# A fused recurrence and mish MLP on one core: 64-column state updates, VectorE low parts for 16 units, and a new planned order

## The chip, the cores and the metric

The kernel runs on one core of a Trainium2 chip. The metric is the device time of one execution in microseconds (us). The kernel before takes 505.66 us, the median of three runs (505.22 to 505.91).

## The reference

The inputs are `q`, `k`, `v` and `f_logit` of shape (batch 4, heads 8, 768 steps, width 48), all float32, and two weight matrices, `w_in` (384 x 2048) and `w_out` (2048 x 384), in float64.

```
f = sigmoid(f_logit)
state = 0                                   # per batch and head, 48 x 48
for t in range(768):
    state = f[t][:, None] * state + outer(k[t], v[t])
    y[t]  = q[t] @ state
x = y as (3072 tokens, 8 * 48 = 384)
h = x @ w_in                                # 3072 x 2048
g = h * tanh(softplus(h))                   # mish
out = g @ w_out                             # 3072 x 384
```

## The kernel before

**The recurrence.** Each sequence is cut into 6 blocks of 128 steps, so with 4 batches there are 24 chunks n = 0 to 23; a chunk holds all 8 heads of one batch. Two heads sit on the 128 partitions, 64 places each: 48 numbers in groups of three, each group followed by an empty place (`places` in the host layout, with zeros for v). A chunk is worked in four steps. `prep`/`attn0` make decays and the masked scores (L449, L455), `attn1` transposes k (by TensorE, or from chunk 8 by VectorE and DMA), `attn2` multiplies transposed k by v to get the chunk's two state updates `u[0]` and `u[1]` (L514) and VectorE adds them to the state (`mid` L534, `tmp` L536), and `attn3` makes the outputs y (L553, L565). `leave` brings y into the token layout `xt` in two parts, a rounded high part and the remainder, and GpSimd decays the state (L588).

**The joined runs.** From chunk 9 (`JOIN`) the scores of a chunk, the outputs of the chunk before it and the state update are one uninterrupted TensorE step of small matmuls, 15 runs in all (n = 9 to 23). There the update uses array tiles of 64 rows x 32 columns, 4 pairs of heads x 4 column groups x 2 halves of the chunk. In the last four (n >= 20) only the first half is needed. Each small float32 matmul shows as two matmul records and two weight loads in the trace. The moving operand of the update is v with the empty places left out, a pattern of 16 groups of 3; the other matmuls of the run (L449, L553, L565) move 64 contiguous columns.

**The MLP.** Tokens are taken in 6 groups of 512, the 2048 hidden features in 16 blocks: 96 units. A unit has 9 matmuls h = xt x w_in (L245; three products of high and low parts for each of three row blocks), an elementwise chain (`mish`), and 9 matmuls o = w_out x g (L271). The chain of a unit: ScalarE L259, VectorE L260, ScalarE L256, L262, L263, VectorE g (L264), ScalarE the high part gh (L265), GpSimd the low part gl = g - gh (L266). Units 0 to 15 are feature blocks 0 to 7 of groups 0 and 1; units 16 to 31 are blocks 8 to 15 of the same groups (`TURNS`). `split_w` turns one block's float64 weights, loaded as pairs of 32-bit words, into high and low parts with ScalarE (L357, L364) and VectorE (L359, L360, L362, L365), one block for each of units 0 to 7 and 16 to 23.

**The order.** Nothing runs at the place where the code names it. Every step is added to `Plan` with its engine, a cost, and what it reads and writes. `order` packs the steps onto five in-order queues by a list schedule, forward and backward in turns (`BASE`: look-ahead, weight of waiting, number of turns), perturbs the ranks with each seed of `SEEDS`, packs once more, and issues all steps in the order of their planned starts. Steps marked `port` (SBUF-only VectorE steps, and all of GpSimd's) are planned so that they do not overlap. `FREE` gives each engine's first free time; the order of its keys decides which engine is taken when two steps could start at the same time. Before the first MLP output, small matmuls on zeros (`idle`, L345) fill planned TensorE gaps.

Of the kernel before, what the change touches and what calls it, by code (L numbers as in the profile page):

```python
# [10 lines left out]
F32 = mybir.dt.float32  # L11
# [3 lines left out]
ALU = mybir.AluOpType  # L15
PSUM = bass.MemoryType.PSUM

B, H, S, D = 4, 8, 768, 48
# [6 lines left out]
NP = H // 2  # L25
NS = 4
GC = B
GT = GC * C
# [11 lines left out]

LEAD = [(-4, 4), (24, 32)]
SEEDS = [
# [4 lines left out]
]  # L47
BASE = (600.0, 20.0, 2)
NR = 3
LAG = 2  # L50
TD = 8
# [1 line left out]
KD_SIZE = 131.0  # L53
RAW = 786
SQ_DVE = ()


class Plan:
# [4 lines left out]

    LATENCY = {"pe": 230.0, "act": 170.0, "dve": 160.0, "pool": 180.0, "sp": 1550.0}
    RATE = 0.385
    FREE = {"pe": 1500.0, "act": 1900.0, "dve": 1200.0, "pool": 2100.0, "sp": 600.0}

    def __init__(self):
        self.steps = []
# [16 lines left out]
    def pack(self, rank, ahead, haste, back=False):  # L86
# [10 lines left out]
        if back:  # L97
            before, after = after, before
        free = dict.fromkeys(self.FREE, 0.0) if back else dict(self.FREE)
        queue = {e: [] for e in free}  # L100
# [54 lines left out]
    def order(self):  # L155
        count = len(self.steps)
        cost = [s[1] for s in self.steps]
        ahead, haste, turns = BASE
        rank = list(range(count))
# [9 lines left out]
    def issue(self):  # L169
        at = self.FREE["pe"]  # L170
        for i in self.order():
            engine, cost, issue = self.steps[i][:3]
            if engine == "pe":

                if self.start[i] <= self.start[self.until]:
                    while at + 527.0 < self.start[i]:
                        self.idle()
                        at += 427.0 if at > 6500.0 else 853.0
                at = self.start[i] + cost
            issue()  # L180
# [8 lines left out]
def T_ACT(n, psum=False, bias=0):  # L189
    return n / 1.2 + (50 if psum else 92) + 93 * bias + 2  # L190


def T_DVE(n):
    return n / 0.96 + 70


def T_POOL(n):
    return n * 2.3 + 60
# [3 lines left out]
def recurrence_moe_kernel(  # L202
# [12 lines left out]
    nc = tc.nc  # L215
# [32 lines left out]
                n += 1  # L248


    def mish(h, n, g, gh, gl, on_dve=False):


        square = (
            ("dve", T_DVE(GT), 1, lambda: nc.vector.tensor_tensor(n, n, n, ALU.mult)) if on_dve else
            ("act", T_ACT(GT), 0, lambda: nc.scalar.activation(n, n, AF.Square))  # L256
        )
        return (
            ("act", T_ACT(GT, True), 0, lambda: nc.scalar.activation(n, h, AF.Exp)),  # L259
            ("dve", 70 + GT / 1.92, 1, lambda: nc.vector.tensor_scalar(n, n, U_CAP, 1.0, ALU.min, ALU.add)),  # L260
            square,
            ("act", T_ACT(GT, False, 1), 0, lambda: nc.scalar.activation(n, n, AF.Ln, bias=ones)),  # L262
            ("act", T_ACT(GT), 0, lambda: nc.scalar.activation(n, n, AF.Exp, scale=-1.0)),  # L263
            ("dve", 662, 0, lambda: nc.vector.scalar_tensor_tensor(g, n, half_, h, ALU.subtract, ALU.mult)),  # L264
            ("act", T_ACT(GT), 0, lambda: nc.scalar.activation(gh, g, AF.Copy)),  # L265
            ("pool", T_POOL(GT), 1, lambda: nc.gpsimd.tensor_tensor(gl, g, gh.bitcast(F32), ALU.subtract)),  # L266
        )

# [7 lines left out]
    with tc.tile_pool(name="work", bufs=1) as pool, tc.tile_pool(  # L276
        name="psum", bufs=1, space=PSUM
    ) as psum:
        def ring(name, n, shape, dtype=F32, space=pool):
            return [space.tile(shape, dtype, tag=f"{name}{i}", name=f"{name}{i}") for i in range(n)]  # L280
# [9 lines left out]
        n_, g_ = (ring(nm, 2, [P, GT]) for nm in "ng")  # L290
        gh_, gl_ = (ring(nm, 3, [P, GT], F32R) for nm in ("gh", "gl"))
# [3 lines left out]
        at_, h_, o_ = (ring(nm, n, [P, GT], F32, psum) for nm, n in (("at", 3), ("h", 2), ("o", NK)))  # L295
# [41 lines left out]
        at1, zeros = at_[2], o_[NK - 1]  # L337
# [87 lines left out]
        def half(e):  # L425
            return slice(64 * e, 64 * e + 64)
# [4 lines left out]
        def real(x):  # L431
            return x.rearrange("x p (r m) -> x (p r) m", m=4)[:, :, 0:3]
# [59 lines left out]
        def attn2(n):  # L492
            last = n >= NCH - B
            st, ks = state[:, n % B], ("st", n % B)
            v = v_[n % NR]
            join = n >= JOIN
            u = [x[:, c : c + NP * D].rearrange("p (a c) -> p a c", a=NP) for x, c in ((at1, 0), (at_[1], NP * 64))]
            keys = [("at", 2), ("at", 1)]
            if join:
                u.reverse()  # L500
                keys.reverse()
            flat = [x.rearrange("x p (r m) -> x (p r) m", m=3) for x in u]
            (mid, mk), (tmp, tk) = ((r[n % 2], (nm, n % 2)) for nm, r in (("mid", mid_), ("tmp", tmp_)))

            kt = kt_[n % 2]

            def update():
                m = 32 if join else 64
                for p in range(NP):
                    for r in range(0, P, m):  # L510
                        for c in range(2 - last):
                            c0 = 2 * p * 64 + r // 64 * 64
                            moving = v[half(c), c0 : c0 + 64].rearrange("x (r m) -> x r m", m=4)[:, :, 0:3]
                            nc.tensor.matmul(u[c][r : r + m, p, :], kt[half(c), p, r : r + m], moving, start=True, stop=True)  # L514

            if join:
                scores, mask, reads, writes = late[n]
                outputs, qreads, after = ahead[n - 1]
                add("pe", 2300, lambda: [scores(), outputs(), update()], [("kt", n % 2), ("v", n % NR)] + reads + qreads,
                    [("at", b) for b in range(3)])  # L520
                after()
                mask()
            elif n >= GC:
                scores, mask, reads, writes = late[n]
                add("pe", 1190, lambda: [update(), scores()], [("kt", n % 2), ("v", n % NR)] + reads,
                    list(dict.fromkeys(keys[: 2 - last] + writes)))
                mask()
            else:
                add("pe", 640, update, [("kt", n % 2), ("v", n % NR)], keys[: 2 - last])
            if n < B:  # L530
                add("act", T_ACT(NP * D, True), lambda: nc.scalar.activation(real(mid), flat[0], AF.Copy),
                    keys[:1], [mk])
            else:
                add("dve", T_DVE(NP * D), lambda: nc.vector.tensor_tensor(real(mid), real(st), flat[0], ALU.add), keys[:1] + [ks], [mk])  # L534
            if not last:
                add("dve", T_DVE(NP * D), lambda: nc.vector.tensor_tensor(real(tmp), flat[1], real(mid), ALU.add), keys[1:] + [mk], [tk])  # L536
# [79 lines left out]


        steps = (attn0, attn1, attn2, attn3)

        def attend():  # L620
# [75 lines left out]
        for u in range(len(units) + LAG):  # L696
            if u < len(units):
                t, g, j = units[u]
                if j == split:
                    split_w(j)  # L700
                    split += 1
                x, hs, us, gs = g % 2, u % 2, u % 2, u % 3
                xk = [(hl, ("xt", x, c), p) for hl in "hl" for c in range(GC) for p in range(NK)]
                h = h_[hs]
                add("pe", 2050, lambda h=h, x=x, j=j: moe_in(h, xt_[x], j), xk + [("w", "h", j), ("w", "l", j)], [("h", hs)])
                kh, kn, kg = ("h", hs), ("n", us), ("g", us)
                ops = mish(h, n_[us], g_[us], gh_[gs], gl_[gs], u in SQ_DVE)
                rw = (
                    ([kh], [kn]), ([], [kn]), ([], [kn]), ([], [kn]), ([], [kn]),
                    ([kh, kn, "half_"], [kg]), ([kg], [("gh", gs)]), ([kg, ("gh", gs)], [("gl", gs)]),  # L710
                )
                for (e, c, shared, fn), (r, w) in zip(ops, rw):
                    add(e, c, fn, r, w, port=shared)
            while done < min(4 * NCH, attend_goal(u) + 3 * (JOIN < NCH)):
                attend()
            if u == len(units):
                check()
            if u >= LAG:
                out_unit(u - LAG)
# [8 lines left out]
    with tc.If(good < total):  # L728
# [3 lines left out]
        with tc.tile_pool(name="slow", bufs=1) as pool, tc.tile_pool(  # L732
            name="slow_psum", bufs=1, space=PSUM
        ) as psum:
            def st(shape, name):
                return pool.tile(shape, F32, tag=name, name=name)
# [5 lines left out]
            with tc.For_i(0, B, 1) as b:  # L742
                with tc.For_i(0, NP, 1) as p:
# [15 lines left out]
                    with tc.For_i(0, D, 1) as e:  # L759
                        v = st([P, S], "sv")  # L760
# [24 lines left out]
            with tc.For_i(0, NG, 1) as g:  # L785
                x = st([P, NK, GT], "sx")
# [10 lines left out]
                n, g_ = (st([P, GT], nm) for nm in ("sn", "sg"))  # L797
                gh, gl = (pool.tile([P, GT], F32R, tag=nm, name=nm) for nm in ("sgh", "sgl"))
# [87 lines left out]
```

## Time and profile before

| What | Value |
|---|---|
| Median of 3 runs | 505.66 us |
| The profiled execution, its own time | 507.56 us |
| Its span, first to last instruction | 505.8 us |
| Mean granted TensorE clock, as a share of full speed | 0.990 |
| TensorE matmul busy | 485.6 us (96%) |
| ScalarE busy | 396.9 us (78%) |
| VectorE busy | 304.1 us (60%) |
| GpSimd busy | 155.2 us (31%) |

In the profile PE is TensorE's matmuls, PEld its weight loads, DVE VectorE, ACT ScalarE, POOL GpSimd and SPq the queue of SyncE that issues the transfers. The profile's times count from the first instruction. Busy shares are averages over stretches with different limits, so the rows further down are taken stretch by stretch.

### The profile page before, as it was taken

To read this page: it belongs to the slowest core of one execution; us is meant where nothing else is said; L and a number is where in the kernel's file an instruction comes from. 1 tells how busy PE (TensorE), PEld (TensorE's weight loads), DVE (VectorE), ACT (ScalarE), POOL (GpSimd) and SP (SyncE) were. 2 spreads that over 40 slices of the span, in tenths; PEclk is the share of its full clock that TensorE was granted. 3 is DMA by queue.
4 is the path that set the end of the run, shared out by engine and by line. 5 is a ranking of instruction groups with operands and counts; after the bars stand their busy time and mean duration, and the time that the engine had idled before them with its cause. 6 is when DMAs were issued, how large, how long until landed. Compare 5 with 4: busy or idle time off the path is not lost.

```text
span 505.8 us, 13416 instructions
## 1 busy us (share of the span) xinstructions
PE 485.6 (96%) x5594; PEld 394.0 (78%) x5594; DVE 304.1 (60%) x512; ACT 396.9 (78%) x714; POOL 155.2 (31%) x138
## 2 busy tenths in 40 slices
PE   7998999998999989999999999999999999999995
PEld 5766777776788877888888888888888888888883
DVE  3997999999846855577466366456365433233221
ACT  6996998888998876498877878877877777777680
POOL 3121354332433313142322332322332333342421
PEclk8998999999999999999999999999999999999998
DMA  8876556453142462643233252233141100100001
GB/s 300 305 259 220 182 183 194 153 172 131 48 145 61 125 182 76 194 110 75 74 86 101 69 153 74 69 75 100 50 134 22 24 32 1 43 21 1 0 1 67
DMA packets 55379, 54.53 MB, mean 108 GB/s; under 512 B 36976, under 2 KB 38128, under 8 KB 55312
## 3 DMA queue, kind: packets, MB, share of 16 engines
q1 hardware_dynamic: 55312, 53.63, 34.8%
q8 instruction: 44, 0.72, 0.6%
q14 instruction: 23, 0.19, 0.1%
HBM read 40.76 MB, written 10.49 MB: 101 GB/s over the span
## 4 chain that ended last, share of the span: by engine, by line
PE 76%; DVE 10%; ACT 7%; issue 3%; DMA 1%; POOL 1%; SPq 1%; DVEq 0%; ACTq 0%; POOLq 0%
PE o L271 34%; PE h L245 33%; PE at L514 2%; PE at L565 2%; PE at L449 2%; DVE wt L362 2%; PE at L553 2%; DVE g L264 1%; DVE wt L360 1%; DVE kq L312 1%; DVE wl L365 1%; DVE n L260 1%; DVE cum L409 1%; ACT wt L357 1%; DVE wt L359 1%
## 5 line engine op out<-in xcount | busy, mean ns | idle before, releaser
L266 POOL TENSOR_TENSOR gl<-g,gh 128x512 fp32r<-128x512 f32 x96 | 131.3, 1369 | 299.0 <-ACT gh L265 268.0
L245 PE MATMUL h<-xt,wh 128*128 128x512 f32 x576 | 181.3, 396 | 7.6 <-DVE g L264 4.8
L245 PEld LDWEIGHTS h<-xt,wh 128*128 128x128 f32 x576 | 107.2, 189 | 34.0 <-DVE g L264 8.8
L264 DVE SCALAR_TENSOR_TENSOR g<-n,half,h 128x512 f32<-128x512 f32 x96 | 71.4, 744 | 74.9 <-ACT n L263 68.5
L271 PE MATMUL o<-gh,wh 128*128 128x512 f32 x288 | 114.0, 396 | 0.0
L245 PE MATMUL h<-xt,wl 128*128 128x512 f32 x288 | 112.7, 391 | 0.0
L271 PE MATMUL o<-gh,wl 128*128 128x512 f32 x288 | 112.2, 390 | 0.0
L271 PE MATMUL o<-gl,wh 128*128 128x512 f32 x288 | 112.2, 390 | 0.0
L259 ACT ACTIVATE n<-h 128x512 f32<-128x512 f32 x96 | 56.9, 592 | 49.6 <-PE h L245 49.3
L260 DVE TENSOR_SCALAR n<-n 128x512 f32<-128x512 f32 x96 | 44.8, 468 | 70.1 <-ACT n L259 69.7
L256 ACT ACTIVATE n<-n 128x512 f32<-128x512 f32 x96 | 60.5, 630 | 16.6 <-DVE n L260 16.4
L262 ACT ACTIVATE n<-n,ones 128x512 f32<-128x512 f32 x96 | 69.4, 723 | 2.7
L265 ACT ACTIVATE gh<-g 128x512 fp32r<-128x512 f32 x96 | 60.0, 625 | 12.7 <-DVE g L264 10.8
L271 PEld LDWEIGHTS o<-gh,wh 128*128 128x128 f32 x288 | 54.0, 188 | 12.4 <-ACT n L256 0.4
L245 PEld LDWEIGHTS h<-xt,wl 128*128 128x128 f32 x288 | 54.5, 189 | 11.7
L271 PEld LDWEIGHTS o<-gl,wh 128*128 128x128 f32 x288 | 54.1, 188 | 11.5
L271 PEld LDWEIGHTS o<-gh,wl 128*128 128x128 f32 x288 | 54.1, 188 | 10.8
L263 ACT ACTIVATE n<-n 128x512 f32<-128x512 f32 x96 | 60.3, 628 | 1.8
L312 DVE TENSOR_TENSOR kq<-kq,at 128x512 f32<-128x512 f32 (+1 forms) x39 | 26.0, 668 | 2.4 <-ACT at L417 1.4
L409 DVE TENSOR_TENSOR_SCAN cum<-go,l 128x512 f32<-128x512 f32 x20 | 26.1, 1304 | 0.0
L455 DVE TENSOR_TENSOR a<-at,causal 128x256 f32<-128x256 f32 x44 | 17.9, 413 | 13.4 <-PE at L514 13.4
L514 PE MATMUL at<-v,kt 64*32 64x48 f32 (+1 forms) x1120 | 19.5, 214 | 2.6 <-issue 2.6
(104 smaller groups left out, 451.7 us busy)
## 6 DMA issues: line engine op xcount, KB each, us to landing
raw<-ww SPq DMA_DIRECT2D x16, 768.0 KB, 4.9
kq<-kq SPq DMA_DIRECT2D x63, 128.0 KB, 3.2
v<-vn SPq DMA_DIRECT2D x24, 256.0 KB, 3.4
l<-fl SPq DMA_DIRECT2D x20, 256.0 KB, 2.8
out<-ob SPq DMA_DIRECT2D x18, 256.0 KB, 2.9
kd<-inv SPq DMA_DIRECT2D x64, 64.0 KB, 2.2
kt<-kd SPq DMA_DIRECT2D x16, 256.0 KB, 2.7
xt<-xt SPq DMA_DIRECT2D x15, 128.0 KB, 2.1
```

The source lines that it names most:

```text
L245: nc.tensor.matmul(h, w[:, j, a * P : (a + 1) * P], xt[:, x, a, :], start=(n == 0), stop=(n == 3 * NK - 1))
L256: ("act", T_ACT(GT), 0, lambda: nc.scalar.activation(n, n, AF.Square))
L259: ("act", T_ACT(GT, True), 0, lambda: nc.scalar.activation(n, h, AF.Exp)),
L260: ("dve", 70 + GT / 1.92, 1, lambda: nc.vector.tensor_scalar(n, n, U_CAP, 1.0, ALU.min, ALU.add)),
L262: ("act", T_ACT(GT, False, 1), 0, lambda: nc.scalar.activation(n, n, AF.Ln, bias=ones)),
L263: ("act", T_ACT(GT), 0, lambda: nc.scalar.activation(n, n, AF.Exp, scale=-1.0)),
L264: ("dve", 662, 0, lambda: nc.vector.scalar_tensor_tensor(g, n, half_, h, ALU.subtract, ALU.mult)),
L265: ("act", T_ACT(GT), 0, lambda: nc.scalar.activation(gh, g, AF.Copy)),
L266: ("pool", T_POOL(GT), 1, lambda: nc.gpsimd.tensor_tensor(gl, g, gh.bitcast(F32), ALU.subtract)),
L271: nc.tensor.matmul(o, w[:, j, m * P : (m + 1) * P], x, start=(first and i == 0), stop=(last and i == 2))
L312: add("pool" if on_pool else "dve", cost, lambda: eng.tensor_tensor(dst, x, y, ALU.mult), reads, writes, port=port)
L409: add("dve", 2 * T_DVE(w) - 70, lambda s=s, cum=cum: nc.vector.tensor_tensor_scan(cum.rearrange("p a c -> p (a c)"), go[:, s].rearrange("p ...
```

## The change

Four things. (1) In joined runs the update's moving operand is all 64 columns of a head's v, empty places included, the PSUM target is 64 columns wide for each pair, and VectorE reads it back without the empty places. (2) For units 0 to 15 VectorE makes gl in place of GpSimd. (3) In `FREE` GpSimd stands ahead of VectorE, and `BASE` has 6 turns in place of 2. (4) `SEEDS` is another list, of 50 in place of 31, so that the order of all engines' instructions is another one. Planned costs of the joined run (2300) stay as they were.

```diff
-    62000004, 62000073, ...            (31 seeds)
+    71000002, 71000010, ...            (50 seeds)
-BASE = (600.0, 20.0, 2)
+BASE = (600.0, 20.0, 6)
+LOW_DVE = range(16)
-    FREE = {"pe": 1500.0, "act": 1900.0, "dve": 1200.0, "pool": 2100.0, "sp": 600.0}
+    FREE = {"pe": 1500.0, "act": 1900.0, "pool": 2100.0, "dve": 1200.0, "sp": 600.0}
-    def mish(h, n, g, gh, gl, on_dve=False):
+    def mish(h, n, g, gh, gl, on_dve=False, low_on_dve=False):
             ("act", T_ACT(GT), 0, lambda: nc.scalar.activation(gh, g, AF.Copy)),
+            ("dve", T_DVE(GT), 1, lambda: nc.vector.tensor_tensor(gl, g, gh.bitcast(F32), ALU.subtract)) if low_on_dve else
             ("pool", T_POOL(GT), 1, lambda: nc.gpsimd.tensor_tensor(gl, g, gh.bitcast(F32), ALU.subtract)),
-            u = [x[:, c : c + NP * D].rearrange("p (a c) -> p a c", a=NP) for x, c in ((at1, 0), (at_[1], NP * 64))]
+            cols = 64 if join else D
+            u = [x[:, c : c + NP * cols].rearrange("p (a c) -> p a c", a=NP) for x, c in ((at1, 0), (at_[1], NP * 64))]
-            flat = [x.rearrange("x p (r m) -> x (p r) m", m=3) for x in u]
+            flat = [real(x) if join else x.rearrange("x p (r m) -> x (p r) m", m=3) for x in u]
-                            moving = v[half(c), c0 : c0 + 64].rearrange("x (r m) -> x r m", m=4)[:, :, 0:3]
+                            moving = v[half(c), c0 : c0 + 64]
+                            if not join:
+                                moving = moving.rearrange("x (r m) -> x r m", m=4)[:, :, 0:3]
-                ops = mish(h, n_[us], g_[us], gh_[gs], gl_[gs], u in SQ_DVE)
+                ops = mish(h, n_[us], g_[us], gh_[gs], gl_[gs], u in SQ_DVE, u in LOW_DVE)
```

## Rows read from the trace of the kernel before

**Rows 1.** Busy time by stretch: PE, PEld, DVE, ACT, POOL, granted clock, DMA share, GB/s.
```profile
40.00:50.00 10.00, 9.85 (x111) 7.67 (x112) 6.44 (x13) 6.37 (x12) 1.76 (x2) 0.83 0.73 251
50.00:75.00 25.00, 24.96 (x510) 19.61 (x508) 23.63 (x44) 23.89 (x47) 11.31 (x9) 1.00 0.57 186
75.00:131.50 56.50, 51.72 (x457) 39.69 (x438) 54.42 (x70) 47.89 (x81) 20.04 (x14) 1.00 0.51 157
131.50:495.40 363.90, 361.31 (x3840) 298.24 (x3840) 187.50 (x333) 284.51 (x501) 110.34 (x91) 1.00 0.26 73
```

**Rows 2.** What TensorE waited for in all: total us, times, longest.
```profile
PE h L245 <- DVE g L264: 4.8, 9, 0.8
PE h L245 <- DMA xt<-xt: 2.8, 1, 2.8
PE at L514 <- issue: 2.6, 2, 1.5
```

**Rows 3.** Timeline of TensorE's matmuls in the joined run of chunk 15.
```profile
248.28 0.69 PE L449 MATMUL at<-kq 64*64 64x64 f32 x32
...
249.87 0.96 PE L514 MATMUL at<-v,kt 64*32 64x48 f32 x64
...
250.77 0.50 PE L271 MATMUL o<-gh,wh 128*128 128x512 f32 x1
```

**Rows 4.** Line L565 by shape in 249.59 to 249.86 us; line L514 of that run.
```profile
L565 PE MATMUL at<-a,v 64*32 64x64 f32 x32 | 0.5, 222 | 0.0
...
L514 PE MATMUL at<-v,kt x64: 199/203/225, 249.9 to 250.6; 64*32 64x48 f32 x64
```

**Rows 5.** Timeline of the joined run of chunk 20, its update and what follows.
```profile
345.09 0.62 PE L514 MATMUL at<-v,kt 64*32 64x48 f32 x32
345.64 0.50 PE L271 MATMUL o<-gh,wh 128*128 128x512 f32 x1
```

**Rows 6.** Timeline of a joined run with a pause inside its update.
```profile
178.70 0.69 PE L449 MATMUL at<-kq 64*64 64x64 f32 x32
...
180.29 0.64 PE L514 MATMUL at<-v,kt 64*32 64x48 f32 x38
182.41 0.38 PE L514 MATMUL at<-v,kt 64*32 64x48 f32 x26 [1.48 <-issue]
```

**Rows 7.** DMA queues of the page: packets, MB, share of 16 engines.
```profile
q8 instruction: 44, 0.72, 0.6%
```

**Rows 8.** VectorE's groups in 75 to 131.5 us: count, busy us, mean ns.
```profile
L365 DVE TENSOR_TENSOR wl<-wt,wh 128x768 fp32r<-128x768 f32 x7 | 9.8, 1405 | 0.0
L360 DVE SCALAR_TENSOR_TENSOR wt<-raw,wt 128x768 int32<-128x768 int32 x8 | 9.8, 1225 | 0.1
L260 DVE TENSOR_SCALAR n<-n 128x512 f32<-128x512 f32 x12 | 8.5, 712 | 0.0
L362 DVE SCALAR_TENSOR_TENSOR wt<-raw,wt 128x768 int32<-128x768 int32 x7 | 7.7, 1104 | 0.0
L359 DVE TENSOR_SCALAR wt<-wt 128x768 int32<-128x768 int32 x7 | 5.0, 707 | 0.1
```

**Rows 9.** The tiles wl and gl in 40 to 140 us: ns min/median/max.
```profile
L365 DVE TENSOR_TENSOR wl<-wt,wh x12: 927/953/2051, 44.6 to 135.5; 128x768 fp32r<-128x768 f32 x12
L266 POOL TENSOR_TENSOR gl<-g,gh x18: 1297/1342/2218, 50.3 to 137.5; 128x512 fp32r<-128x512 f32 x18
```

**Rows 10.** Timelines of POOL, then DVE, at 82 to 86 us.
```profile
82.87 1.75 POOL L266 TENSOR_TENSOR gl<-g,gh 128x512 fp32r<-128x512 f32 x1 [2.63 <-ACT gh L265]
...
82.52 0.95 DVE L362 SCALAR_TENSOR_TENSOR wt<-raw,wt 128x768 int32<-128x768 int32 x1
83.39 2.05 DVE L360 SCALAR_TENSOR_TENSOR wt<-raw,wt 128x768 int32<-128x768 int32 x1
```

**Rows 11.** VectorE's groups by shape: in 10 to 40 us, in 200 to 495, over the span.
```profile
L359 DVE TENSOR_SCALAR wt<-wt 128x768 int32<-128x768 int32 x5 | 2.8, 554 | 0.1
...
L260 DVE TENSOR_SCALAR n<-n 128x512 f32<-128x512 f32 x64 | 27.3, 427 | 59.7 <-ACT n L259 59.3
...
L312 DVE TENSOR_TENSOR kq<-kq,inv 128x256 f32<-128x256 f32 x2 | 0.8, 421 | 2.9 <-ACT inv L416 2.9
L455 DVE TENSOR_TENSOR a<-at,causal 128x256 f32<-128x256 f32 x44 | 17.9, 413 | 13.4 <-PE at L514 13.4
L534 DVE TENSOR_TENSOR mid<-state,at 128x192 f32<-128x192 f32 x20 | 6.9, 344 | 0.0
```

**Rows 12.** Timeline of TensorE at the first MLP unit.
```profile
40.16 0.74 PE L245 MATMUL h<-xt,wh 128*128 128x512 f32 x2 [2.76 <-DMA xt<-xt]
```

9 rows, old and new, of the table SEEDS are left out of this document.

## The prediction

> **What bounds the kernel now.** I read the page's busy shares first, then the table by stretch, then TensorE's waits, then single joined runs, then VectorE's groups in the one stretch where TensorE starves. The reader is to see four stretches. Up to 40 us the first chunks of the recurrence are worked, and the first MLP matmul starts at 40.16 after a wait for the copy inside xt [rows 12]. From 40 to 75 us TensorE is nearly full while VectorE has 10.00 - 6.44 = 3.6 and 25.00 - 23.63 = 1.4 us idle [rows 1]. From 75 to 131.5 us VectorE is busy 54.42 of 56.50 us and TensorE idles 56.50 - 51.72 = 4.8 us; the release named is VectorE's g, which frees the bank of h [rows 1, 2]. From 131.5 to 495.4 us TensorE is full: 361.31 of 363.90 us, and all but half a microsecond of the rest are two pauses inside state updates that no engine explains, 2.6 us together [rows 1, 2]. VectorE has more than 170 us to spare there. So a microsecond of TensorE work taken out after 131.5 us should arrive at the end whole; a microsecond of VectorE work counts only between 75 and 131.5 us; GpSimd, at 110 of 364 us in the long stretch, counts only through what it holds up.
>
> **The update with 64 columns.** Before, a run's update is 64 matmul records, from 249.87 to the next matmul at 250.77: 0.90 us [rows 3]. Just ahead of it the same array shape, 64 x 32, moves 64 contiguous columns in 32 records in 0.27 us, 8.4 ns apart, with the filling of the array after a change of shape counted in [rows 4]. The update's last record starts at 249.87 + 0.96 - 0.20 = 250.63 (the last ones take 0.20) [rows 3, 4], so its records start 0.76 / 64 = 11.9 ns apart, and 0.14 us go to the change to the full array. So 48 columns in groups of three are slower than 64 in one piece. At 8.4 ns the update would be 64 x 8.4 + 140 = 0.68 us, 0.22 less; without the filling, which does not recur as the shape stays, the records of Rows 4 can come at 7 ns (estimate), 0.59 us, 0.31 less. The other end is that the update is paced by columns: 0.76 x 64 / 48 = 1.01, 0.25 more. I take 0.28 less, nearest to the row with the same array shape, the same v tile and contiguous columns.
>
> [...] The rows differ: the gapped 48 columns take 11.9 ns a record, the contiguous 64 take 8.4. [...]
>
> Of the 15 runs, chunk 9's lies near 125 us where VectorE is the limit: nothing. Chunks 10 to 19: 10 x 0.28 = 2.8 less. Two of them carry the pauses and may give nothing: 2.2. Chunks 20 to 23 use one half of the rows, 32 records from 345.09 to 345.64, 0.55 us [rows 5]; with half the array's tiles their records can come at about 14 ns, 32 x 14 + 140 = 0.59: 4 x 0.04 = 0.2 more. Together -2.0 to -2.6; taken: -2.4. VectorE's read of PSUM with gaps is not shown; L534 takes 344 ns for 192 columns with one gapped operand, and L455 413 ns for 256 whole ones [rows 11]. So 0 to 70 ns for 26 reads, under 2 us, all hidden under VectorE's spare time after 131.5 us; if that cover were gone it would be those 2 us. Bounds for the part: -3.2 and +3.2 (2.5 plus 4 x 0.17).
>
> **gl on VectorE for units 0 to 15.** Removed from GpSimd: 16 instructions of 1.34 us [rows 9]. Added to VectorE: 16 of 128x512 with both inputs in SBUF. Such a multiply of 256 columns takes 421 ns [rows 11], a subtraction of 768 columns 927 at best [rows 9]; in between, 421 + 256 x (927 - 421) / 512 = 0.67 us. Sixteen are 10.8 us on the engine that limits the front. But VectorE is now held up by these very GpSimd instructions: L360 takes 2.05 us while gl runs, against 0.95 for the like L362 just before it [rows 10]. In 75 to 131.5 us the excess is L365 7 x (1.405 - 0.927) = 3.3, L360 8 x (1.225 - 0.95) = 2.2, L362 7 x (1.104 - 0.95) = 1.1, L260 12 x (0.712 - 0.427) = 3.4, L359 7 x (0.707 - 0.554) = 1.1: 11.1 us [rows 8 to 11]. Twelve units pass there (L260 x12), so 12 x 0.67 = 8.0 come on: net 3.1 us less for VectorE. The other four, 2.7 us, fall before 75 us, into its 5.0 us idle. [...]
>
> An added wait comes along: gl on VectorE waits for ScalarE's gh, and behind it in the same queue stand the weight steps and the next unit's g, on which TensorE's next h waits. The order must put other work between g and gl; where it doesn't, each unit costs its gh. Bounds for TensorE: -4.8 (all its idle there) and +8.0 (all twelve on the path, no hold removed). I take -2.0, near the net of the rows with a third off for such waits. GpSimd's queue has the state decays and the later gl left; nothing in it is late.
>
> **The order, `FREE`, `BASE`, the seeds.** These cost no instruction, but all five queues, SP's transfers too, stand in another order. In the long stretch an order that keeps TensorE full gives nothing. [...] No row favours a side: 0, from -4 to +4.
>
> **The sum.** The profiled execution is 507.56: 507.56 - 2.4 - 2.0 = 503.2. It lies 1.9 above the median of 505.66, so in medians 505.66 - 4.4 = 501.3.
>
> **The rivals.**
> - Instruction fetch (other side). A joined run is 176 matmul records (32 + 32 + 48 + 64) and as many weight loads, 352 instructions, in 2.5 us; the instruction queue moved 0.72 MB in 44 packets, 16 KB each [rows 7]. The pause at 180.73 lies inside such a run with nothing to wait for [rows 6], so I read it as code that came late; 1.5 and 1.1 us. The new order shifts where a run lies against these pieces, and a faster update uses them up sooner. Each further paused run costs 1.3 and its gain of 0.28, 1.6; slower than before from four more on: 501.3 + 4 x 1.6 = 507.7. With no pause left: 501.3 - 2.6 - 0.6 = 498.1. For it: runs are alike, so neighbours may pause together. Against: 13 of 15 show none. [...]
> - VectorE pays. If the holds fall by less than 8.0 - 2.4 = 5.6 of the 11.1 us, the added work eats the shorter update; with no relief, 505.66 - 2.4 + 8.0 = 511.3; with half, 505.66 - 2.4 + 8.0 - 5.5 = 505.8. Against it: the hold in Rows 10 stands beside gl and nothing else.
> - 64 columns cost by the column: 505.66 + 3.2 - 2.0 = 506.9. Against it: Rows 4.
> - The order also takes most of the front's idle: another 3 to 4.8 from VectorE and xt: about 497.5.
> - The order loses 4: 505.3.
>
> **How the numbers follow.** Forecast (499 to 504): 0.50. Order or fetch win (495 to 499): 0.18. Fetch loses (505 to 509): 0.13. VectorE pays (505 to 511): 0.07. Order loses (503 to 508): 0.07. Columns cost: 0.05. A difference under 0.2%, 1 us, can't be told from none. Faster: 0.48 + 0.18 + 0.02 + 0.01 + 0.02 = 0.71; same 0.13; slower 0.16. The range leaves the ends of the first win and of the losses out: 496.5 to 507.0.
>
> **What would show it.** Right: records of L514 in joined runs from chunk 10 about 7 to 8.4 ns apart, 0.6 to 0.7 us to the next matmul; L266 on DVE 16 times near 0.67 us; means of L360, L362, L365 near 0.95 in the front and L260 near 0.43; less TensorE idle on L264 before 131 us; as many pauses as before. Wrong: updates of 0.9 us or more; VectorE still at 96% with TensorE idle over 4.8 us before 131 us; more than four joined runs with a pause of over 1 us; a first h matmul much later than 40 us.

## The result and the profile after

The changed kernel takes 499.84 us, the median of four runs (498.42 to 501.06), against 505.79 for the kernel before beside it (505.22 to 506.21): a ratio of 0.9882, interval 0.9853 to 0.9911. The forecast was 501.3 us. So 5.95 us are gone where 4.4 were expected, but they did not all come from where they were expected.

The table by stretch of the changed kernel answers to [rows 1]; columns are PE, PEld, DVE, ACT and POOL busy with counts, granted clock, DMA share, GB/s:

```profile
40.00:50.00 10.00, 8.98 (x120) 6.71 (x113) 9.76 (x18) 9.17 (x19) 1.80 (x2) 1.00 0.83 287
50.00:75.00 25.00, 25.00 (x512) 19.98 (x512) 24.62 (x46) 24.25 (x47) 5.89 (x5) 1.00 0.51 168
75.00:131.50 56.50, 54.07 (x461) 44.46 (x460) 53.34 (x84) 51.63 (x87) 3.99 (x3) 1.00 0.51 162
131.50:488.00 356.50, 355.19 (x3810) 292.97 (x3809) 191.26 (x330) 280.52 (x493) 107.38 (x89) 1.00 0.26 74
```

From 75 to 131.5 us TensorE idles 2.4 us in place of 4.8 (1.3 of the 2.4 are a pause in chunk 9's update), GpSimd is busy 4.0 us in place of 20.0, and 40 to 50 us is run at full clock in place of 0.83. The count of MLP matmuls between 40 and 131.5 us tells what that is worth. First the kernel before, then the changed one (line, shape, count, busy us, mean ns, idle time before with what ended it):

```profile
L245 PE MATMUL h<-xt,wh 128*128 128x512 f32 x108 | 36.5, 421 | 7.1 <-DVE g L264 4.3 <-DMA xt<-xt 2.8
L245 PE MATMUL h<-xt,wl 128*128 128x512 f32 x54 | 21.7, 401 | 0.0
L271 PE MATMUL o<-gh,wh 128*128 128x512 f32 x42 | 16.7, 397 | 0.0
```

```profile
L247 PE MATMUL h<-xt,wh 128*128 128x512 f32 x120 | 37.9, 397 | 1.0 <-DVE g L266 1.0
L247 PE MATMUL h<-xt,wl 128*128 128x512 f32 x59 | 23.0, 390 | 0.0
L274 PE MATMUL o<-gh,wh 128*128 128x512 f32 x46 | 18.2, 397 | 0.0
```

The three o groups are equal in number, so 108 + 54 + 3 x 42 = 288 matmuls were done by 131.5 us before, and 120 + 59 + 3 x 46 = 317 are done now. At the 0.227 us from the start of one to the start of the next in a full stretch, 29 matmuls are 6.6 us. The span fell by 505.8 - 498.5 = 7.3 us. So nine tenths of the gain is made before 131.5 us. The other 0.7 us lies behind: of the two pauses in updates one now lies before 131.5 us, which is more than the longer updates cost. The two profiled executions are not quite alike, either: the one before took 507.56 us, 1.9 above its median, the one after 500.22, 0.4 above.

TensorE's waits, rows of the view (total us, times, longest), answer to [rows 2]:

```profile
PE at L520 <- issue: 2.3, 2, 1.3
PE at L407 <- ACT l L404: 2.2, 2, 1.7
...
PE h L247 <- DVE g L266: 1.0, 1, 1.0
...
PE h L247 <- DMA xt<-xt: 0.2, 1, 0.2
```

The wait for VectorE's g fell from 4.8 to 1.0 us, the one for xt from 2.8 to 0.2; two pauses in updates ("issue": the engine waited for nothing that the profile shows) are there as before.

The updates, in chunk 15's run and in chunk 20's, answer to [rows 3, 5]:

```profile
242.11 0.99 PE L520 MATMUL at<-v,kt 64*32 64x64 f32 x64
243.03 0.50 PE L274 MATMUL o<-gh,wh 128*128 128x512 f32 x1
...
337.44 0.73 PE L520 MATMUL at<-v,kt 64*32 64x64 f32 x32
338.09 0.50 PE L274 MATMUL o<-gh,wh 128*128 128x512 f32 x1
```

From the update's first matmul to what follows it is 0.92 us (0.90 before) and 0.65 (0.55 before). The 64 columns made the update longer. VectorE's groups from 75 to 131.5 us and the tile gl answer to [rows 8, 9]:

```profile
L268 DVE TENSOR_TENSOR gl<-g,gh 128x512 fp32r<-128x512 f32 x12 | 8.2, 679 | 0.0
L363 DVE SCALAR_TENSOR_TENSOR wt<-raw,wt 128x768 int32<-128x768 int32 x7 | 6.7, 953 | 0.1
L365 DVE SCALAR_TENSOR_TENSOR wt<-raw,wt 128x768 int32<-128x768 int32 x7 | 6.7, 950 | 0.0
L368 DVE TENSOR_TENSOR wl<-wt,wh 128x768 fp32r<-128x768 f32 x6 | 5.7, 944 | 0.0
L262 DVE TENSOR_SCALAR n<-n 128x512 f32<-128x512 f32 x12 | 5.1, 423 | 1.5 <-ACT n L261 1.4
L362 DVE TENSOR_SCALAR wt<-wt 128x768 int32<-128x768 int32 x8 | 4.8, 601 | 0.0
```

The low part takes 0.68 us on VectorE (0.67 estimated). The weight steps L363, L365, L368 and the step L262 of the chain are at 0.95, 0.95, 0.94 and 0.42 us; the same steps, L360, L362, L365 and L260 before, had 1.23, 1.10, 1.41 and 0.71. L362, the shift of the weights, is at 0.60 where it had 0.71 (L359).

### The profile page after: what moved, and what is told of

Read it like the earlier page. It is cut to its first block, busy times and chain, and to the rows that moved or that the text cites. A ratio compares the mean times of both kernels' runs of the same rounds, so it can differ in the third digit from the quotient of the medians.

```text
span 498.5 us, 13401 instructions
## 1 busy us (share of the span) xinstructions
PE 481.1 (97%) x5588; PEld 392.8 (79%) x5588; DVE 308.0 (62%) x528; ACT 397.5 (80%) x714; POOL 132.9 (27%) x122
## 4 chain that ended last, share of the span: by engine, by line
PE 81%; DVE 7%; DMA 5%; SPq 2%; ACT 2%; issue 1%; POOL 0%; DVEq 0%; POOLq 0%; ACTq 0%
PE o L274 36%; PE h L247 35%; PE at L520 3%; PE at L571 2%; PE at L452 2%; DMA l<-ft 2%; PE at L559 2%; DMA kq<-kq 1%; DVE wt L365 1%; DMA raw<-ww 1%; DVE g L266 1%; SPq L385 1%; DVE wt L363 1%; DMA kd<-inv 1%; DVE gl L268 1%
## 5 line engine op out<-in xcount | busy, mean ns | idle before, releaser
L269 POOL TENSOR_TENSOR gl<-g,gh 128x512 fp32r<-128x512 f32 x80 | 106.8, 1340 | 303.1 <-ACT gh L267 280.2
L247 PE MATMUL h<-xt,wh 128*128 128x512 f32 x576 | 179.4, 393 | 1.3 <-DVE g L266 1.0
L262 DVE TENSOR_SCALAR n<-n 128x512 f32<-128x512 f32 x96 | 45.9, 478 | 70.5 <-ACT n L261 70.0
L412 DVE TENSOR_TENSOR_SCAN cum<-go,l 128x512 f32<-128x512 f32 x20 | 27.4, 1369 | 0.3 <-ACT l L404 0.3
L520 PE MATMUL at<-v,kt 64*32 64x64 f32 (+1 forms) x1120 | 20.2, 224 | 4.7 <-issue 2.3
```

The costliest lines, as they stand in the source:

```text
L247: nc.tensor.matmul(h, w[:, j, a * P : (a + 1) * P], xt[:, x, a, :], start=(n == 0), stop=(n == 3 * NK - 1))
L412: add("dve", 2 * T_DVE(w) - 70, lambda s=s, cum=cum: nc.vector.tensor_tensor_scan(cum.rearrange("p a c -> p (a c)"), go[:, s].rearrange("p ...
```

## The experiments

Each kernel was compared with the kernel before on the same chip; its median there was 507.24 us beside the first four, 507.12 beside the next four, 506.57 beside the last two. Experiments 4 and 5 were timed once and are read from their traces.

**1. The update's columns alone.**

```diff
 the changed kernel
-            cols = 64 if join else D
+            cols = D
...
-            flat = [real(x) if join else x.rearrange(...) for x in u]
+            flat = [x.rearrange(...) for x in u]
...
-                            if not join:
-                                moving = moving.rearrange(...)[:, :, 0:3]
+                            moving = moving.rearrange(...)[:, :, 0:3]
```

> The changed kernel with the update's moving operand back at 48 columns in groups of three; every engine's order as in the changed kernel. In the changed kernel's trace a 64-column update takes 0.925 us to the next matmul (0.656 in the last four runs) against 0.895 and 0.55 before. Theory A, the columns and their gaps don't pace the update: updates go back to 0.90 and 0.55, the time falls by 10 x 0.03 + 4 x 0.11 = 0.7 us, to about 499.1. Theory B, the step of my prediction (64 whole columns are faster, and the new order hides it): updates get longer than 0.925, the time rises by 2 us or more, to 502 or above.

Measured: 499.25 us (499.01 to 500.49), ratio to before 0.9847 (0.9816 to 0.9878). The updates of chunks 15 and 20:

```profile
242.66 0.95 PE L519 MATMUL at<-v,kt 64*32 64x48 f32 x64
243.54 0.50 PE L274 MATMUL o<-gh,wh 128*128 128x512 f32 x1
...
337.88 0.62 PE L519 MATMUL at<-v,kt 64*32 64x48 f32 x32
338.43 0.50 PE L274 MATMUL o<-gh,wh 128*128 128x512 f32 x1
```

0.88 and 0.55 us again. Theory A holds: the order of all engines is the same, and with 48 gapped columns the update of chunk 15 is 0.04 us shorter, 0.03 on the average of the full ones, and those of the last four 0.11. The median is 0.6 us below the changed kernel's, as expected, but a difference of that size is not told from none between chips; the durations in the trace are what shows it. By them this part of the change costs about 0.7 us.

**2. The new order with the low parts on GpSimd.** One word in the planned step of VectorE, so that the order stays (the 64 columns stay too):

```diff
-            ("dve", T_DVE(GT), 1, lambda: nc.vector.tensor_tensor(gl, ...)) if low_on_dve else
+            ("dve", T_DVE(GT), 1, lambda: nc.gpsimd.tensor_tensor(gl, ...)) if low_on_dve else
```

> The changed kernel, same planned order, but the low parts of units 0 to 15 are issued on GpSimd again. Theory A, the holds between GpSimd and VectorE made the front slow: VectorE's weight steps go back to means of 1.1 to 1.4 us in 75 to 131.5 us, TensorE idles 4 us or more there, and the time rises by 5 to 8 us, to 505 to 508. Theory B, the new order made the front fast: TensorE stays as full as in the changed kernel and the time rises by 1 us at most, to 499 to 501.

Measured: 502.14 us (501.57 to 503.72), ratio 0.9905 (0.9873 to 0.9937). VectorE's weight steps and the stretch, 75 to 131.5 us:

```profile
75.00:131.50 56.50, 53.87 (x454) 43.32 (x454) 53.28 (x71) 51.54 (x89) 21.63 (x14) 1.00 0.51 162
...
L363 DVE SCALAR_TENSOR_TENSOR wt<-raw,wt 128x768 int32<-128x768 int32 x7 | 10.0, 1425 | 0.1
L365 DVE SCALAR_TENSOR_TENSOR wt<-raw,wt 128x768 int32<-128x768 int32 x7 | 8.6, 1230 | 0.1
```

Between the theories. The holds are back in full (1.43 and 1.23 us), yet TensorE idles only 2.6 us there (1.6 of them the pause in chunk 9's update), and the time is 2.3 us above the changed kernel's 499.84 by the medians, 1.2 by the ratios to before (0.9905 less 0.9882, of 507), not 5 to 8. VectorE's holds no longer reach TensorE in this order: h waits 0.9 us for g, and 114 + 57 + 3 x 46 = 309 MLP matmuls are done by 131.5 us, 21 or 4.8 us more than before. The order and the 64 columns, with GpSimd still making the low parts, are worth 507.24 - 502.14 = 5.1 us by the medians (4.8 by the ratio, interval 3.2 to 6.4). With the 0.7 us that the columns cost, the order is worth 5.8. It is an order planned for low parts on VectorE.

**3. The old order with the low parts on VectorE.**

```diff
 the kernel before
-            ("pool", T_POOL(GT), 1, lambda: nc.gpsimd.tensor_tensor(gl, ...)),
+            ("pool", T_POOL(GT), 1, lambda: (nc.vector if low_on_dve else nc.gpsimd).tensor_tensor(gl, ...)),
-                ops = mish(..., u in SQ_DVE)
+                ops = mish(..., u in SQ_DVE, u < 16)
```

> The kernel before, same planned order, but the low parts of units 0 to 15 are issued on VectorE at the places where the order has GpSimd's. Theory A (the holds): VectorE's weight steps fall to means of 0.95 us in the front, the time falls by 3 to 6 us, to 500 to 503. Theory B (the order): in an order made for GpSimd the 16 x 0.68 us on VectorE cost what the holds gave, within 1 us of 505.8.

Measured: 502.12 us (501.06 to 505.51), ratio 0.9912 (0.9876 to 0.9947). The stretch 75 to 131.5 us, VectorE's steps in it, and TensorE's wait over the whole span:

```profile
75.00:131.50 56.50, 55.39 (x461) 43.94 (x460) 54.43 (x88) 52.46 (x88) 1.93 (x3) 1.00 0.51 157
...
L362 DVE SCALAR_TENSOR_TENSOR wt<-raw,wt 128x768 int32<-128x768 int32 x8 | 7.6, 954 | 0.0
L360 DVE SCALAR_TENSOR_TENSOR wt<-raw,wt 128x768 int32<-128x768 int32 x8 | 7.6, 953 | 0.1
...
PE h L245 <- DVE g L264: 1.5, 3, 0.7
```

Theory A: with nothing but the engine changed, 5.1 us are gained by the medians (4.5 by the ratio, interval 2.7 to 6.3). VectorE is exactly as busy as before (54.43 against 54.42 us), but for more work: the weight steps are 0.95 us in place of 1.10 to 1.23, and the low parts fill the room. The wait of h on g falls from 4.8 to 1.5 us. One thing in this trace bears on the reading of the first result:

```profile
40.00:50.00 10.00, 9.43 (x117) 7.37 (x117) 8.78 (x17) 8.25 (x17) 1.94 (x2) 1.00 0.83 285
...
PE h L245 <- DMA xt<-xt: 1.0, 1, 1.0
```

In the old order, too, 40 to 50 us is run at full clock and the wait for xt is 1.0 us, though the low parts begin only at 49 us. So the 2.8 us wait and the clock of 0.83 in [rows 1, 2] belong at least in part to that one execution and not to its order.

**4. Forms of the update, one for each joined run.**

```diff
 the changed kernel
-                for p in range(NP):
-                    for r in range(0, P, m):
-                        for c in range(2 - last):
+                loops.sort(key=lambda x: [x["prc".index(i)] for i in form[2]])
...
-                add("pe", 2300, lambda: [scores(), outputs(), update()], ...)
+                add("pe", 2300, lambda: [x() for x in {..., "first": (update, scores, outputs), ...}[form[0]]], ...)
```

> The changed kernel, but the update of each joined run has another form. Loops outer to inner, p pair of heads, r group of 32 columns of the array, c half of the rows: chunks 10 and 19 p r c as in the change, 11 r p c, 12 p c r, 13 c p r, 14 c r p, 17 r c p, 16 p r c with 48 columns; 15 (64 columns) and 18 (48) with the update first in the run; of the last four, with one half only, 20 update first, 21 r p c, 22 48 columns, 23 as in the change. Theory A, the update is paced by how its weight loads and matmuls take turns on the tiles, not by columns: 48 and 64 columns differ by 0.05 us at most in the same place, while loop orders differ by 0.1 us or more, and the two halves one after the other (c first) are slowest, near 1.1. Theory C, the queue of TensorE is drained by the matmuls before it: the update at the head of the run, behind slow full-array matmuls, takes 64 records at 7 to 8.4 ns, 0.45 to 0.55 us, whatever its columns, and what then stands last gets slower. Theory B, columns: 48 columns are slower than 64 in each place.

Measured once: 503.15 us. From the update's first matmul to the next other one, in us:

| Chunk | Form | us |
|---|---|---|
| 10, 19 | p r c, 64 columns, as in the change | 0.91, 0.93 |
| 16 | p r c, 48 columns | 0.88 |
| 13 | c p r | 0.97 |
| 11 | r p c | 1.40 |
| 14, 17 | c r p; r c p | 2.31; 2.31 |
| 15 | p r c, 64 columns, at the head of the run | 0.79 |
| 18 | p r c, 48 columns, at the head of the run | 0.74 |
| 20, 21, 22, 23 | one half: at the head; r p c; 48 columns; as in the change | 0.58; 1.29; 0.55; 0.66 |

Chunk 12 (p c r, 2.12) holds one of the pauses and tells nothing. A tile of the array is one c with one r; the four p share it. Where successive matmuls stay on one tile (p innermost; with one half, r p c too), or only two tiles take turns (r p c), the update is 1.5 to 2.5 times as long. Where four or eight tiles take turns, 64 columns in place of 48 cost 0.03 to 0.05 us of 0.9 in the full updates. In the half updates, on four tiles, they cost 0.11 of 0.55, more than theory A allowed. So theory A holds for the full updates, though its guess on which order is slowest was wrong: c first with r innermost is 0.97, not near 1.1. Theory C was right for half of the update. The run of chunk 15, its update at the head; then line L531 counted in 241.50 to 241.78 us:

```profile
241.54 0.86 PE L531 MATMUL at<-v,kt 64*32 64x64 f32 x64
242.32 0.39 PE L458 MATMUL at<-kq 64*64 64x64 f32 x10
...
L531 PE MATMUL at<-v,kt 64*32 64x64 f32 x32 | 0.5, 222 | 0.0
```

The first 32 records start within 0.24 us (241.54 to 241.78), 7 ns apart or a little more; the other 32 take 0.54 us to the next shape. Exactly 32 pairs of weight load and matmul, 64 instructions, come fast behind the full-array matmuls, and then no more. Chunk 18's update shows the same 32. On four tiles it does not hold: in chunk 20, its half update also at the head, less 0.15 us for the change of shape behind it (0.148 between the last record on 64 x 64 tiles and the first on 64 x 32 in chunk 15's run before, 249.457 to 249.605 us), (0.58 - 0.15) / 32 makes 13 to 14 ns a record. In the run as it is ordered, the 32 records of line L565, on which I built the price, are those 32: they stand behind that change of the array's shape, 6 to 9 ns apart but for one step of 33, and the update behind them gets the slow rate. No run changes what stands in TensorE's queue alone, so that the queue is their cause, as theory C has it, is not shown. Putting the update first moves the fast ones, but it adds a change of shape, and the run as a whole is as long: 0.79 + 0.52 + 0.47 + 0.73 = 2.50 us against 2.52.

**5 and 6. Where the pauses come from.** In the kernel before, the changed one and experiments 1 to 4, counting two instructions for each matmul record, every pause in an update begins at instruction 154 to 162, modulo 256. Some instructions that change no result were added, at a place where TensorE fills time with zeros (one such matmul, 4 instructions, gives way to 6 or 14 small ones of 4 each):

```diff
         def idle():
+            idles.append(0)
+            if len(idles) == 5:
+                for i in range(6):                     # 14 in experiment 6
+                    r = 32 * (i % 4)
+                    nc.tensor.matmul(zeros[r : r + 32, 0:64], state0[0:64, r : r + 32], state0[0:64, 0:64], start=True, stop=True)
+                return
             nc.tensor.matmul(zeros[:, : 2 * P], state0[:, 0:P], state0, start=True, stop=True)
```

> The changed kernel with 20 more TensorE instructions near 12 us (one of the matmuls on zeros gives way to 6 small ones on one array tile each, of the same length together). Every pause inside an update, in the kernel before, the changed one and the four runs so far, begins at TensorE's instruction 154 to 162 counted modulo 256. Theory A, it is a border between 16 KB pieces of code, and a run pauses when it holds two borders and the first lies 36 to 98 instructions into the run: the pauses of chunks 9 and 12 move 10 records to the front, from after the 57th and 54th update record to after the 47th and 44th; no other appears; the time stays within 1 us of 499.8. Theory B, the pauses belong to the place in the order (a transfer, a full queue): they stay at the 57th and 54th record.

> As the one before with 52 more instructions (14 small matmuls in place of one). Theory A (code borders): the first border of the runs of chunks 9 and 12 falls 30 instructions into the run, as in chunk 11 of the changed kernel, which does not pause: both pauses vanish, chunk 13's second border lies just behind its run; 2.3 to 2.6 us less, 497.2 to 497.6. Theory B: pauses and time as in the changed kernel, 499.8.

Chunk 9's update in the changed kernel, then those of chunks 9 and 12 with 20 instructions more:

```profile
127.26 0.93 PE L520 MATMUL at<-v,kt 64*32 64x64 f32 x57
129.49 0.31 PE L520 MATMUL at<-v,kt 64*32 64x64 f32 x7 [1.30 <-issue]
```

```profile
125.91 0.84 PE L528 MATMUL at<-v,kt 64*32 64x64 f32 x47
127.87 0.35 PE L528 MATMUL at<-v,kt 64*32 64x64 f32 x17 [1.11 <-issue]
...
189.85 0.74 PE L528 MATMUL at<-v,kt 64*32 64x64 f32 x44
191.98 0.41 PE L528 MATMUL at<-v,kt 64*32 64x64 f32 x20 [1.39 <-issue]
```

20 instructions are 10 records, and the pauses moved from after the 57th and 54th record to after the 47th and 44th, to the record. Its one time was 499.07 us. With 52 more, both are gone, as theory A has it, and theory B is out:

```profile
125.38 1.02 PE L528 MATMUL at<-v,kt 64*32 64x64 f32 x64
126.34 0.50 PE L247 MATMUL h<-xt,wh 128*128 128x512 f32 x1
...
PE at L528 <- issue: 1.4, 1, 1.4
```

But one came up after the 61st record of chunk 13's update, which I had put just behind its run. The median is 498.71 us (498.05 to 502.38; ratio 0.9854, interval 0.9818 to 0.989), short of the 497.2 to 497.6 expected and not told from the changed kernel's own (0.9882, or 0.9844 in experiment 10).

The count above leaves out the semaphore instructions, and a few others, that stand among TensorE's own. With them counted from the start of each trace, every pause in a joined run's update, wherever the traces have one, falls at the same place, instruction 192 or 193 modulo 256; call it a border. The new one in chunk 13 does so too. The twelve traces hold 180 joined runs. A full one is 352 instructions and can hold two borders 256 apart. All 19 full runs with the first border 44 to 91 instructions in pause for 1.0 to 1.8 us, always at the second border; of the other 161 none holds a pause of over 0.2 us at a border, also where the first lies 31 or 39 in. That the code of the next piece comes late there is my reading: it fits, but no trace shows the load itself.

**7. Both together.** The edits of 1 and 6 in one kernel.

> Both together: 52 more instructions near 12 us and the update with 48 gapped columns, on the changed kernel's order. If the two add: 499.8 - 0.7 - 2.4 = 496.7. If the pauses stay or the columns give nothing: 499.1 to 499.8, or 497.4.

Measured: 497.35 us (496.34 to 500.83), ratio 0.983 (0.9792 to 0.9867). It is 1.4 below experiment 6 on the same chip and near the 496.7 of the sum. That sum took 2.4 us for the pauses, but this trace holds the pause in chunk 13's update too ("PE at L527 <- issue: 1.4, 1, 1.4"); so the nearness is in part chance, and the columns' 0.7 explain half of the 1.4.

**8. The new plan with the old seeds.**

```diff
 the changed kernel
-    71000002, 71000010, ...            (50 seeds)
+    62000004, 62000073, ...            (31 seeds)
-BASE = (600.0, 20.0, 6)
+BASE = (600.0, 20.0, 2)
-    FREE = {..., "pool": 2100.0, "dve": 1200.0, ...}
+    FREE = {..., "dve": 1200.0, "pool": 2100.0, ...}
```

> The changed kernel (low parts of 16 units planned on VectorE, 64 columns), but with the seeds, the number of turns and the key order of the kernel before: the order is planned anew and nothing has fitted those seeds to it. Theory A, moving the low parts is worth 4 to 5 us in any order and the fitted order 3: about 502 to 503. Theory B, an order that isn't fitted loses everything: 505 or above.

Measured: 509.44 us (508.13 to 510.99), ratio 1.0054 (1.0026 to 1.0081): theory B by the time. My reading is that moving the low parts in the plan changes every start, and the old seeds then perturb a plan that they were not chosen for. The stretch and two of TensorE's waits:

```profile
50.00:75.00 25.00, 23.30 (x372) 18.23 (x372) 24.58 (x40) 22.17 (x41) 4.00 (x4) 1.00 0.44 146
75.00:131.50 56.50, 53.63 (x421) 42.36 (x420) 54.64 (x90) 50.59 (x88) 2.58 (x1) 1.00 0.54 171
...
PE at L519 <- issue: 3.3, 2, 2.3
PE h L246 <- DVE g L265: 2.4, 3, 1.4
```

TensorE loses 1.7 us between 50 and 75 us and 2.9 between 75 and 131.5, together about the 4.8 of the kernel before, with VectorE as full. Chunk 9's joined run, whose update starts at 144.59 us here and at 125.30 before, comes 19 us later. Of the 3.3 us of pauses only 1.0 lies in a joined run; 2.3 is one in an update near 19 us. So a plan made anew under settings that were fitted to another one loses what the engine change gives in the old order (experiment 3); the changed kernel's own settings make it faster. Whether the seeds alone, the six turns or the key order do it wasn't tried apart.

**9 and 10. Another shift, beside the changed kernel.** Experiment 7 with 12 small matmuls in place of 14, and the changed kernel unaltered.

> 48 columns and 44 more TensorE instructions near 12 us. With 52 one pause was left, in chunk 13, after the 61st record; with 44 its second border lies at instruction 354 of 352, behind the run. The first border of the runs of chunks 9 and 12 falls 38 instructions into the run: 30 did not pause (chunk 11 of the changed kernel), 42 did (chunk 11 of the kernel before). If 38 is early enough: no pause of over 1 us in any update, 1.4 us less than with 52 and 48 columns on the same chip. If not: two pauses, after the 35th and 32nd record, and 1 us more than with 52.

> The changed kernel once more, beside the one above on one chip, as the base for it: 499.8, pauses after the 57th record of chunk 9's update and the 54th of chunk 12's. The version above should stand 2 to 3 us below it.

Measured: 497.35 us (496.74 to 498.44), ratio 0.9811 (0.9786 to 0.9835), beside 498.93 for the changed kernel (498.05 to 500.54), ratio 0.9844 (0.9818 to 0.987). No update holds a pause of over 1 us, as expected; but chunk 13's has only moved behind its run:

```profile
PE h L247 <- issue: 1.2, 1, 1.2
...
PE at L527 <- issue: 0.8, 2, 0.6
```

The second line is a pause of 0.6 us near 19 us and one of 0.2 after the 35th record of chunk 9's update, the place named for the case that it paused there. So the gain on the changed kernel is 1.6 us, not 2 to 3: 0.7 from the columns and about one of the two pauses. Behind the run that pause is nearly as long (1.2 us) as inside it (1.4 in experiment 6). By its ratio this is the fastest version found, with experiment 7's the same median on another chip; each of its six runs but one is below the changed kernel's lowest. The split in 0.7 and about one is worked out from durations, not measured apart.

## Why the prediction was right, and where it was wrong

**The place of the limit was right.** Most of the time went between 40 and 131.5 us, where TensorE waited for VectorE, and VectorE for GpSimd. After that stretch the update's length and the pauses are the only changes that I found.

**The update's term failed.** The step "I take 0.28 less, nearest to the row with the same array shape, the same v tile and contiguous columns" took the rate of 32 records for that of 64. Here only the first 32 records behind a change of shape or a slower stretch come at that rate (0.24 us for the first 32, 0.54 for the other 32 in experiment 4), and the update stands behind them. In place of -2.4 us the runs showed 10 x 0.03 + 4 x 0.11 = 0.7 us more. The rival that columns pace the update (3.2 more) is wrong for the full runs, where one third more columns cost 3%, but not far off in the last four: 0.11 us each, where it had 0.17. In experiment 1 the 48 gapped columns take 0.88 us and the 64 whole ones 0.92, against my reading of [rows 4]; no run has 48 columns without gaps, which alone would tell the gaps from the columns.

**The engine's term was right in mechanism and too small.** Holds of 11.1 us off, 8.0 on, was the working. That the holds go wholly with their cause was my assumption; the rows after show it nearly so (0.95, 0.95, 0.94, 0.42 and 0.60 us where 1.23, 1.10, 1.41, 0.71 and 0.71 stood), and 8.2 us of low parts. I took 2.0, with a third off for waits on gh; experiment 3 shows 5.1 by the medians in the old order, and against experiment 2 it is 1.2 to 3.1 in the new one (by the ratios of the first result and of experiment 10). No cost of such waits was seen.

**The order's term was mis-sized.** I had 0, from -4 to +4, which no row or run shows. With the low parts kept on GpSimd it is -5.1 with the columns' cost in it, so about -5.8 (experiment 2): h waits 0.9 us for g in place of 4.8. I had not seen that an order alone could take that wait, except as a rival. The shorter wait for xt (0.2 us there) and the full clock at 40 to 50 us are not shown to be the work of the order: experiment 3, in the old order, has 1.0 us and the full clock as well. By the median the term lies outside my bound of -4; the interval, 3.2 to 6.4 with the columns in, doesn't settle it. The two gains are not additive: 5.1 each without the other, 6.0 and 7.6 together (the first result, and experiment 10's 498.93 against 506.57), since both take away the same wait for g.

**The fetch rival's pauses were real but neutral.** Two pauses before (2.6 us), two after (2.3 us). They sit at one place of the count modulo 256, to the record; that late code makes them is my reading. I had the price right (1.3 taken, 1.0 to 1.8 measured) and did not forecast the count, though the list of instructions would have given it, counted modulo 256. The sum beside it slips by one: three more paused runs, 501.3 + 3 x 1.6 = 506.1, would already be slower than before, not four.

**The sum** came out within 1.5 us by luck: a gain that wasn't there (2.4, in truth 0.7 lost) stood against two that were larger than taken. Engine and order together gave 5.95 + 0.7 = 6.7 us where the sum had 2.0.

## What to carry to other kernels

Price a burst of small matmuls by a burst of its own length: here only the first 32 of 64 came fast. An instruction moved off a slow engine can pay even on a full one, where its cost there is less than what it held up (here 8.2 us against 11.1); and two remedies for the same stall do not add (here 5.1 us each alone, 6.0 to 7.6 together). Where an uninterrupted run pauses with nothing to wait for, its place in the count of the engine's instructions is worth checking, since a few instructions more can remove a pause (52 more took away two here, though one came up elsewhere).

## What the runs showed of the hardware that was not expected

- On eight 64 x 32 tiles in turn, 32 pairs of weight load and matmul start 7 to 8 ns apart behind a slower stretch or a change of the array's shape, the next ones about 12 ((0.54 - 0.15) / 32 in experiment 4, (0.92 - 0.15) / 64 in the changed kernel); 48 gapped or 64 whole columns make 0.03 to 0.05 us of 0.9, but 0.11 of 0.55 on four tiles. What sets the slower rate is open: the forms tried show only that staying on one tile makes it slower still, 36 ns a record (2.31 us for 64).
- A pause inside a joined run lasts 1.0 to 1.8 us, falls at instruction 192 or 193 modulo 256 in every trace that has one, and moves by one record for each two instructions put ahead of it (20 instructions, 10 records).
- A VectorE weight step beside GpSimd's low part loses nearly all of the time that the two overlap: in [rows 10] gl runs to 84.62 us, and L360 starts at 83.39 and takes 2.05, so 1.10 longer than the 0.95 undisturbed, of an overlap of 1.23. The means are 1.43 and 1.23 us against 0.95 in the same order (experiment 2, the changed kernel).
- The changed kernel's first MLP matmul started at 40.0 us in one execution and at 38.5 us in another (experiment 10). Executions of one kernel differ by about 1% here (503.5 to 509.15 us for the kernel before on one chip), so that differences under 1 us rest on the traces, not on medians.
